# A chunked recurrence and its two-layer network: fewer transfers for N's blocks and y's last rows, one transfer queue, and another order of all steps

## The chip, the cores and the metric

The kernel runs on one core of one Trainium2 chip. The metric is the device time of one execution in microseconds (us). The engines' names in the profile are PE (TensorE, matrix products; PEld is its loading of weights), DVE (VectorE), ACT (ScalarE), POOL (GpSimd) and SP (SyncE, which here only issues transfers). SPq and ACTq are transfers as SyncE and ScalarE issue them.

## The reference

A recurrence over 768 time steps runs for 4 batches of 8 heads, each with a state of 40x40. Its outputs are laid side by side, 320 for each of the 3072 tokens, and go through two weight matrices with an exact GELU between them. The weights w_in and w_out arrive as 64-bit floats.

```python
for t in range(S):
    kt, vt, rt = (k[:, :, t], v[:, :, t], r[:, :, t])
    wt, at, bt = (w[:, :, t], a[:, :, t], b[:, :, t])
    y[:, :, t] = np.einsum('bhd,bhde->bhe', rt, state)
    Sa = np.einsum('bhde,bhe->bhd', state, at)
    state = state * wt[:, :, None, :] - np.einsum('bhd,bhe->bhde', Sa, bt) + np.einsum('bhd,bhe->bhde', vt, kt)
x = y.transpose(0, 2, 1, 3).reshape(B * S, H * D)          # 3072 x 320
h = x @ w_in                                               # 320 x 2048
out = (0.5 * h * (1.0 + erf(h / sqrt(2)))) @ w_out         # 2048 x 320
```

## The kernel before

**Chunks.** The 768 time steps are cut into 12 chunks of C = 64. Within a chunk the recurrence becomes matrix products and the inverse of a triangular 64x64 matrix for each head and batch; between chunks only the state is carried (`st`).

**Steps.** Each piece of a chunk's work is a generator, named by a few letters and the chunk. `w`, `a`, `b`, `k`, `v`, `r`, `vp`, `wq`, `bp` and `kp` load inputs (the last four, and `a` and `r` of the later chunks, by `fetch_pairs`); `logs`, `sums`, `wt` and `sc` make the decays; `ta`, `tb`, `tk`, `tv`, `tr` and `tn` turn operands; `N`, `RV`, `A` and `av` are products and masks; `QY` and `qk` add up the rows of y and the next state; `y`, `state`, `X`, `M`, `sa`, `saT` follow from them. `ph` (L1119) is x@w_in with Gelu and `po` (L1141, L1157) the product with w_out; they make up most of TensorE's time. `wi`, `wl` and `wo` load the weights, `ci` and `co` convert them to 32 bits on VectorE (L457 to L473) and ScalarE. `warm` and `begin` are filler products.

**The inverse.** For chunks 1 to 11 it goes this way. `N` takes the product, masks it (L676) and writes it to a DRAM tile (L715). `nb` (L777 to L785) loads its diagonal blocks of 32x32 into `Nb`, twice, for the two halves of the partitions. `inv` substitutes row by row on GpSimd (L799 and the line behind it) and stores the blocks' inverses in DRAM; `ft` (L822, L826) loads them into `Tt`; `corner` turns them on VectorE (L908) and multiplies; `joined` completes the 64x64 inverse. In chunk 0 the same is done by squaring on TensorE, VectorE and ScalarE: `sq` (L865 turns, L868 adds, L871 copies), `cornerd` (L876), `placed` and `joinedd`. `nb` has four transfers: both halves of the partitions for the first sixteen rows of every block, and then, after the next `yield`, both for the last sixteen.

**y.** `y(c)` multiplies the rows by the decays into `xt` (L1045), one head's 40 columns to 64 partitions. `ph` needs x in five pieces of 64 rows: four of them filled with 24 rows from the other half's heads (L1071, three transfers), and a fifth from the 16 rows of each head that are left over (L1076, eight transfers, each of 16 partitions with a stride of 4). For chunk 0 TensorE moves them. For chunk 11, by `MOVED_BY_ACT`, the transfers of one half (x = 1) are issued by ScalarE; all others of the kernel go through SyncE's queue, but for GpSimd's stores of the inverses from chunk 3 on.

**Order.** `ORDER` is a long list of tokens, written out. A token's name says which generator is to take its next step, the figures behind the colons in which pieces of PSUM. The loop at the end takes the tokens one by one:

```python
for token in ORDER.split():
    name, *at = token.split(":")
    places[:] = [int(x) for x in at]
    ...
    next(going[name], None)
```

Each engine, SyncE's queue among them, executes its instructions in the order in which the tokens produce them, and waits where an operand is not there. So the list decides what stands behind what on each engine.

Of the kernel before, what the change touches and what calls it, by code (L numbers as in the profile page):

```python
# [10 lines left out]
FP32 = mybir.dt.float32  # L11
# [8 lines left out]
WORDS_BY_ACT = False  # L20
COPIED_BY_ACT = (1, 2)
MOVED_BY_ACT = (11,)
# [8 lines left out]
w0 begin6 pads1 consts0 w1 tails1 b1 inv1 zeros1 begin6:0 logs0 zeros2 wi0 gaps0 b0 consts0 logs1 tails0 pads0 a0  # L31
consts0 sums0:1 gaps1 sums0:2 zeros0 v0 sums0 zeros4 warm6:3 pads3 pads2 sums1:0 zeros3 shifts0 sums0 sc0 a1 sums1:3
sums1 tb0:2 sums1 sc1 wi0 ta0:1 r0 tb0 ta0 tb1:3 N0:0 N0 tb1 wi0 ta1:2 k0 ta1 N0 tv0:1 sq1 v1 tv0 sq0 N1:3 sq0 sq0:0
sq1 sq0 sq1:2 k1 sq0 sq1 warm1:1 N1 sq1 sk0 ci0:0 wi0 sq1:0 N1 ci0 sq1 tr0:1 sq1 ci0 tk0:2 wi0 tk0 sk1 wi0 sq0:3 sq1
sq0 tr0 A0:2 ci1:1 sq1:0 sq0 ci1 sq1 sq0 nb1 sq1 A0 sq1 wi0 sq0:1 wi0 sq0 RV0:3 sq0 RV0 sq0 wl1 sq1:0 wl1 sq1 inv1 r2
sq0:2 sq1 sq1 sq0 tk1:1 sq0 sq0 sq1:3 tk1 w2 sq1 sq0:0 sq0 cornerd0 placed2 av0:2 ci2:2 placed3 cornerd0:3 ci1 ci2
inv1 nb1 placed1 warm0:1 cornerd0 wl0 ci3:0 wl0 av0 av0:0 r1 ci2 joinedd0:1 av0 joinedd0 tr2:3 placed0 joinedd0 tr2
warm2:2 wi1 a2 ci3 sa0:0 sa0 sa0:1 inv1 sa0 b2 warm5:2 ci4:1 ci9:2 ci4 QY0:3:0 logs2 ci4 k2 qk0 warm7:2 ci9 y0 warm3:1
wi1 state0 wi1 A1:2 wi1 A1 wi1 sums2:1 wi1 inv1 ci9 wo2 sums2:0 sums2 ci3 tv1:3 tv1 tr1:2 sc2 sums2 tn1:0 ci5:1 tn1
ta2:3 ta2 ci5 av1:1 tr1 ci5 sk2 inv1 y0:0 tb2:3 wi1 inv2 ci7:2 tb2 wo6 zeros6 y0:2 ci7 zeros7 y0 y0 tk2:3 av1 ci6:0  # L40
N2:2 ci6 N2 ft1 tk2 co3:1 ph0:0 ft1 ci6 wi1 ph0 corner1:0 N2 ci7 X1:1 corner1:2 corner1 ft1 ph0 X1 ph0:3 wo0 ci8:0
co2:2 ci8 RV1:2 RV1 nb2 warm4:1 ci8 joined1:0 wo9 joined1 wq3 ph0 co0:0 joined1 co0 inv2 ph0 co0 v2 ph0:1 co2 co3
co1:0 sa1:2 co1 sa1 w3 co1 saT1:0 saT1 co3 ph0 co2 wo4 ph0 inv2 ph0:3 co6:0 wt3:1 co6 co7:2 ph0 vp3 co7 ph0 co7
yy1:2:0 logs3 M1:1 M1 tv2:3 wt3 co6 wo8 sums3:1 nb2 sums3 wt3 QY1 zeros5 a3 inv3 tv2 qk1 co4:2 y1 wo15 po0:1 inv2
co5:0 y1 state1 co5 co4 po0 co5 RV2:3 wo10 A2:0 co4 y1 tn2:2 A2 tn2 co9:0 po0 ta3 co9 wt3 inv2 co15:2 bp3 po0 co9 co15
av2:0 co11:1 kp3 co8:0 co11 av2 co11 ph1:2 co8 co8 wo14 inv2 ph1 co10:1 tb3 co10 ph1 wo13 ph1:0 co10 a4 ph1 RV2 ph1
inv4 ft2 co14:0 ph1:2 ta3 co14 wo12 ft2 co14 ft2 N3:3 co15 X2:0 k4 X2 ph1 corner2:1 co13:0 corner2:0 N3 corner2 co13
co12:2 N3 po0 co13 co12 joined2:0 tables0 joined2 k3 joined2 po0 ta4 ph1 co12 sa2:3 nb3 tables0 saT2:0 tk3:1 b3 sa2
sk3 saT2 po0 r3 inv3 yy2:2:3 po0 po0 M2:0 po0 nb3 M2 po0 tv3 ph1:1 inv3 po0 tr3 wq4 ph1 sc3 QY2 w4 qk2 y2 po1:0 state2
bp4 inv3 po1 logs4 b4 A3:2 y2 A3 X3:3 wt4:0 po1 wt4 v3 ph1 wt4 po1 y2 inv3 wt4 po1 po1 ta4 kp4 po1 inv3 vp4 av3:2 tb4  # L50
av3 sums4:1 po1 X3 po1 RV3:2 v4 ws0 sums4 N4:3 N4 inv5 sk4 RV3 ph2:1 N4 sc4 tk4:2 ph2 ft3 ph2 ft3 ph2:3 ws3 nb4 ws1
nb4 ph2 corner3:1 ph2 ft3 ph2:2 inv4 a5 corner3:1 corner3 w5 ph2 ph2 joined3:3 joined3 r4 tn3:1 joined3 tn3 inv4
saT3:3 saT3 sa3:2 sa3 logs5 po1 ph2:1 ta5 bp5 yy3:3:2 M3:0 M3 inv4 tv4 ph2 ph2 tr4 wq5 QY3 qk3 po2:0 po1 sums5:0 sums5
y3 po1 po2:1 state3 y3 po2 inv4 wt5:2 RV4:0 po2:1 po2 wt5 k5 A4:2 po2 A4 tn4:3 y3 tn4 wt5 po2:1 tables1 wt5 po2 po2
inv4 kp5 av4:2 tb5 av4 X4:3 po2 ph3:2 sk5 X4 a6 po2 ta5 ph3 v5 RV4 N5:3 N5 ws2 po2:1 N5 po2 ft4 po2 ph3 ft4 ph3:0 ft4
corner4:0 nb5 tk5:2 ph3 vp5 ph3 corner4:3 ta6 corner4 inv5 nb5 po2 po2:1 po2 joined4:2 joined4 joined4 ph3:0 b5 saT4:3
saT4 sa4:1 r5 inv5 sa4 ph3 ph3 sc5 ph3:2 w6 yy4:3:1 M4:0 M4 tv5 ph3 inv5 ph3 tr5 wq6 QY4 logs6 po3:1 qk4 bp6 state4
po3:0 kp6 y4 po3 po3:2 wt6:0 A5:2 po2 sums6:1 A5 wt6 inv6 k6 inv5 sums6 wt6 y4 po3 wt6 po3 po3:3 po3 po3 tn5:2 y4 tn5
av5:1 tb6 RV5:0 po3 av5 po3 po3:2 ta6 b6 po3 inv5 po3 a7 N6:1 X5:3 N6 X5 N6 sk6 ph4:2 RV5 tk6:1 ph4 ph4 ft5 ta7 ph4:1
ft5 sc6 ft5 A6:3 corner5:0 nb6 r6 inv6 po3 po3:0 po3 corner5:2 A6 corner5 ph4 joined5:0 joined5 ph4 joined5 ph4:2 vp6  # L60
sa5:3 sa5 saT5:0 saT5 inv6 ph4 nb6 ph4 yy5:1:3 w7 M5:0 tr6 tv6 ph4:2 M5 wq7 ph4 inv6 ph4 QY5 v6 logs7 po4:2 qk5 po3 y5
bp7 po4:0 wt7:1 state5 wt7 po4 kp7 po4:0 av6:2 inv7 av6 y5 inv6 wt7 po4 po4 po4:1 wt7 po4 po4 v7 sums7:3 X6:2 y5 po4
ta7 sums7 tb7 po4 po4:0 po4 a8 X6 N7:3 inv6 N7 RV6:1 tk7:2 N7 ph5:2 po4 k7 ph5 ph5 ph5:3 ft6 nb7 ph5 ft6 ph5 nb7
corner6:0 ph5:0 RV6 ft6 inv7 corner6:2 po4 corner6 tn6:3 r7 tn6 po4:1 po4 joined6:2 ta8 joined6 joined6 ph5 inv7 vp7
ph5 sa6:3 sa6 saT6:1 saT6 ph5:2 po4 yy6:0:3 bp8 M6:1 M6 inv7 tr7 ph5 ph5 tv7 QY6 po5:1 wq8 qk6 y6 po5:1 state6 y6 po5
po5:2 inv7 po5 wt8:0 A7:2 y6 RV7:0 A7 wt8 tn7:3 RV7 tn7 wt8 vp8 inv7 po5 po5:1 po5 wt8 po5 X7:2 av7:0 inv8 av7 tb8 sk7
# [12 lines left out]
inv10 po8 wt11 po8:0 av10:2 bp11 po8 wt11 tr10 ph9:1 kp11 ph9 ta11 inv10 ph9 po8 tb11 ph9:0 b10 av10 ph9 X10 sk10 ph9
N11:1 N11 RV10:2 tk11:1 N11 ph9:3 ft10 RV10 ph9 ft10 ph9 nb11 ph9:0 corner10:0 ft10 sc10 w11 ph9 inv11 ph9 corner10:1  # L80
corner10 po9:2 vp11 po9:2 joined10:3 joined10 joined10 po9 nb11 sa10:0 inv11 sa10 r11 saT10:1 po9:1 saT10 tn10:3 tn10
po9 po9 po9:0 yy10:1:3 v11 M10:2 M10 tv11 po9 inv11 po9 po9 logs11 QY10 qk10 y10 po9 po9:2 y10 state10 po9 po9 X11:0
y10 sums11:1 sums11 A11:3 A11 inv11 po9 po9:2 po9 tn11:1 tr11 tn11 av11:3 po9 av11 RV11:2 X11 b11 inv11 RV11 ph10:1
k11 ph10 ph10 sc11 ph10:3 sk11 ft11 ph10 ft11 ph10 ft11 ph10:0 corner11:0 ph10 ph10 corner11:2 corner11 ph10:1
joined11:3 joined11 joined11 ph10 ph10 saT11:0 saT11 po10:2 po10:2 yy11:3:1 M11:0 M11 po10 po10:1 po10 QY11 po10 qk11
y11 po10:0 y11 po10 po10 y11 po10 y11 po10 po10:2 y11 y11 y11 po10 y11 po10 po10 po10:1 po10 po10 ph11:3 ph11 ph11
ph11:0 ph11 ph11 ph11:2 ph11 ph11 ph11:1 ph11 ph11 po11:0 po11:3 po11 po11:2 po11 po11 po11:0 po11 po11 po11 po11
po11:2 po11 po11 po11 po11:1 po11 po11
"""


@with_exitstack
def kernel(
    ctx: ExitStack,
    tc: tile.TileContext,
    r: bass.AP,
# [100 lines left out]

    raws = {}  # L200

    def rows(t):
        return t[:, :G * DM].rearrange("p (g h d) -> p g h d", g=G, h=H)
# [1064 lines left out]
```

## Time and profile before

| | |
|---|---|
| runs of the kernel (us) | 663.88, 664.77, 668.19; median 664.77 |
| span of the profiled execution (us) | 661.8 |
| own time of the profiled execution | not given apart from the span |
| TensorE busy (us) | 646.7 (98%), 13768 instructions |
| TensorE loading weights | 567.3 (86%) |
| VectorE, ScalarE, GpSimd busy | 416.0 (63%), 239.3 (36%), 367.7 (56%) |
| DMA | 300708 packets, 79.41 MB, mean 120 GB/s; SyncE's queue 58.3% of 16 engines' span |
| ScalarE's queue of transfers (y(11), x = 1) | 200 packets, 0.16 MB |

Rows of the timeline have start, duration, engine, line, operation, destination and sources, shapes and count, and in brackets the idle time before them and what ended it. Rows of the waits have the waiting engine and line, what it waited for, and then the total in us, how many times, and the longest. "issue" stands for idle time of an engine that waited for nothing that the profile shows. A row of the stretches has the length of the stretch, each engine's busy time with its number of instructions, the clock that TensorE was granted, the mean busy share of the 16 DMA engines and their GB/s.

### The profile page before, as it was taken

The numbers are of one execution on the slowest core, as the hardware profiler recorded it, in microseconds if no ns is written. First come the engines' busy times: TensorE is split into PE (matmuls) and PEld (weight loads), VectorE is DVE, ScalarE is ACT, GpSimd is POOL, SyncE is SP. The second block draws the span as 40 slices with busy tenths as digits, with TensorE's granted clock in tenths as the row PEclk, the third lists the DMA queues.
The fourth block names the chain that finished last, engine by engine and source line by source line (L and its number), as shares of the span: only waits on it lengthen the run. The fifth ranks groups of instructions, "written<-read, shape, count | busy, mean of one in ns | idle before, by whom it ended". The sixth has DMA issues, their size and how long they took to land.

```text
span 661.8 us, 30753 instructions
## 1 busy us (share of the span) xinstructions
PE 646.7 (98%) x13768; PEld 567.3 (86%) x13768; DVE 416.0 (63%) x536; ACT 239.3 (36%) x305; POOL 367.7 (56%) x799
## 2 busy tenths in 40 slices
PE   8889999999999999999999999999999999999997
PEld 4777788777778988998998998998988999998987
DVE  1778989976483874983863963863765674632313
ACT  4355646432424622522522422515253242232020
POOL 6158536706857837846838836847823874840000
PEclk9999999999999999999999999999999999999999
DMA  9989675696676476764775485675685465450100
GB/s 136 164 192 176 158 167 132 153 159 146 116 132 134 105 137 134 140 116 112 145 141 107 94 153 124 119 147 110 115 146 111 103 121 102 86 101 3 42 1 21
DMA packets 300708, 79.41 MB, mean 120 GB/s; under 512 B 288584, under 2 KB 293328, under 8 KB 300576
## 3 DMA queue, kind: packets, MB, share of 16 engines
q1 hardware_dynamic: 299512, 74.92, 58.3%
q0 software_dynamic: 864, 2.36, 1.8%
q8 instruction: 108, 1.77, 1.1%
q14 instruction: 24, 0.20, 0.1%
q10 hardware_dynamic: 200, 0.16, 0.1%
HBM read 64.09 MB, written 9.70 MB: 112 GB/s over the span
## 4 chain that ended last, share of the span: by engine, by line
PE 82%; DVE 8%; SPq 5%; issue 2%; DMA 1%; ACT 0%; DVEq 0%; ACTq 0%
PE duo L1119 29%; PE duo L149 25%; PE duo L1157 22%; PE duo L1141 4%; PE duo L557 2%; SPq L213 2%; SPq L227 1%; DVE conv L466 1%; SPq L1076 1%; DVE conv L472 1%; DMA spare<-in_a_dram 1%; DVE conv L458 1%; DVE conv L457 1%; DVE aT L588 1%; DMA rows<-in_b_dram 0%
## 5 line engine op out<-in xcount | busy, mean ns | idle before, releaser
L1119 PE MATMUL duo<-xt,w_in_sb 64*128 64x256 f32 x1920 | 218.8, 381 | 1.4 <-issue 1.4
L1119 PEld LDWEIGHTS duo<-xt,w_in_sb 64*128 64x128 f32 x1920 | 182.5, 187 | 23.9 <-issue 2.3
L799 POOL TENSOR_TENSOR tmp<-W,Nb 128x56 f32<-128x56 f32 (+22 forms) x155 | 71.8, 464 | 79.9 <-DMA Nb<-N 51.4
L1122 ACT ACTIVATE gt<-duo 128x1024 f32<-128x1024 f32 x48 | 49.2, 1025 | 143.0 <-PE duo L1119 132.1
L799 POOL TENSOR_TENSOR tmp<-rT,Nb 128x56 f32<-128x56 f32 (+22 forms) x155 | 70.2, 453 | 52.8 <-DMA Nb<-N 41.0
L1157 PE MATMUL duo<-w_out_sb,gt 128*128 128x160 f32 x640 | 93.3, 303 | 0.0
L1157 PEld LDWEIGHTS duo<-w_out_sb,gt 128*128 128x128 f32 x640 | 87.6, 190 | 2.4 <-issue 0.8
L801 POOL TENSOR_TENSOR W<-W,tmp 128x56 f32<-128x56 f32 (+22 forms) x155 | 71.8, 463 | 12.1
L801 POOL TENSOR_TENSOR rT<-rT,tmp 128x56 f32<-128x56 f32 (+22 forms) x155 | 68.4, 441 | 12.1
L1157 PE MATMUL duo<-extra,conv 128*128 128x160 f32 x320 | 46.0, 301 | 0.0
L1157 PEld LDWEIGHTS duo<-extra,conv 128*128 128x128 f32 x320 | 43.8, 190 | 1.4 <-issue 0.5
L1141 PE MATMUL duo<-w_out_sb,gt 128*128 128x320 f32 x128 | 36.9, 440 | 0.1
L1161 DVE TENSOR_TENSOR os<-os,duo 128x160 f32<-128x160 f32 x40 | 12.7, 318 | 31.9 <-PE duo L1157 28.0
L1141 PEld LDWEIGHTS duo<-w_out_sb,gt 128*128 128x128 f32 x128 | 23.6, 190 | 10.1 <-issue 0.5
L1164 DVE TENSOR_TENSOR conv<-gt 128x1024 f32<-128x1024 f32 x10 | 12.7, 1266 | 27.5 <-ACT gt L1122 27.5
L605 POOL TENSOR_TENSOR rows<-rows,w_tile 128x640 f32<-128x640 f32 x9 | 15.8, 1761 | 25.0 <-DMA Nb<-N 16.0
L676 DVE TENSOR_TENSOR SM<-duo,left_upper 128x1024 f32<-128x1024 f32 x11 | 13.4, 1221 | 24.4 <-PE duo L149 24.4
L931 DVE COPY Tt<-duo 32x512 f32<-32x512 f32 x11 | 7.6, 689 | 30.4 <-ACT Tt L931 30.3
L149 PE MATMUL duo<-rT,late 40*64 40x64 f32 x1472 | 26.1, 219 | 0.0
L149 PEld LDWEIGHTS duo<-rT,late 40*64 40x64 f32 x1472 | 23.7, 135 | 2.1 <-issue 2.1
L1122 ACT ACT_TABLE_LOAD x14 | 18.0, 1283 | 19.1 <-DVE os L1161 14.7
L1157 PE MATMUL duo<-extra,gt 128*128 128x160 f32 x160 | 23.9, 302 | 0.0
(222 smaller groups left out, 1092.0 us busy)
## 6 DMA issues: line engine op xcount, KB each, us to landing
Nb<-N SPq DMA_DIRECT2D x40, 128.0 KB
VR<-in_v_dram SPq DMA_DIRECT2D x24, 160.0 KB
out_dram<-os SPq DMA_DIRECT2D x48, 80.0 KB
rows<-in_b_dram SPq DMA_DIRECT2D x22, 160.0 KB
rows<-in_k_dram SPq DMA_DIRECT2D x22, 160.0 KB
w_out_sb<-in_moe_w_out_dram SPq DMA_DIRECT2D x5, 640.0 KB
w_tile<-in_w_dram SPq DMA_DIRECT2D x36, 80.0 KB
Tt<-inv SPq DMA_DIRECT2D x44, 64.0 KB
```

Of the source, the lines that this page charges most:

```text
L149: nc.tensor.matmul(o, lhsT, rhs, start=first, stop=True, skip_group_check=True)
L213: nc.sync.dma_start(out=t[half(e)].rearrange("p g h d -> p (g h) d")[:, :, :D], in_=rows_of(src, c, e))
L557: nc.tensor.transpose(pt[:, g, n], src(g, n), ident)
L605: (nc.gpsimd if c in SCALED_BY_POOL or c >= NB else nc.vector).tensor_tensor(to, raws.pop((c, "k")), t["rw"], ALU.mult)
L676: nc.vector.tensor_tensor(to, pt, upper.unsqueeze(1).to_broadcast([P, NBL, C]), ALU.mult)
L799: eng.tensor_tensor(t, W[:, :nr, j:j + 1].to_broadcast([P, nr, rest]), Nb[:, j:j + 1, j + 1:].to_broadcast([P, nr, rest]), ALU.mult)
L801: eng.tensor_tensor(W[:, :nr, j + 1:], W[:, :nr, j + 1:], t, ALU.add)
L1119: nc.tensor.matmul(pt[:, x, s], w_in_sb[half(x), kt, p * P:(p + 1) * P], xt[half(x), kt], start=kt == 0, stop=kt == NK - 1)
L1122: nc.scalar.activation(gt[:, 4 * q:4 * q + 4].rearrange("p (x s) t -> p x s t", x=2), pt, ACT.Gelu)
L1141: nc.tensor.matmul(pt[:, g], gt[:, f, g * P:(g + 1) * P], w_out_sb[:, f], start=f == 0, stop=f == NF - 1)
L1157: nc.tensor.matmul(pt[:, n, :DM // 2], l_[:, f], r_[:, f], start=f == 0, stop=f == NF // 2 - 1)
L1161: nc.vector.tensor_tensor(to, one_, other, ALU.add)
```

## The change

- `nb`, from chunk 3 on: two transfers instead of four, each with all rows of the blocks for one half of the partitions (4 KB a partition instead of 2).
- `y(c)` for chunks 1 to 10: the fifth piece goes by two transfers into a DRAM tile `last` (16 partitions of 4 KB each) and two back (64 partitions of 1 KB each) instead of eight within the on-chip memory. `y(11)` keeps its eight.
- `WORDS_BY_ACT` and `MOVED_BY_ACT` are gone. Loads and y's transfers go through `load`, whose queue is SyncE's unless a token begins with a star, and none does; so ScalarE's six transfers are SyncE's.
- `fetch_pairs`, `w`, `r`, `N` and `y` yield more often, between single transfers or pairs of them, so that the list can place these apart.
- `ORDER` is another list: 1467 tokens instead of 1334. The computing steps in it are the same, in other places. TensorE has 6976 products before and after; the transfers that SyncE and ScalarE issue go from 780 to 722.

```diff
-WORDS_BY_ACT = False
-MOVED_BY_ACT = (11,)
...
+    raws, queue = {}, [nc.sync]
...
+    def load(out, in_):
+        queue[0].dma_start(out=out, in_=in_)
...
     def nb(c):
...
         for z in range(2):
-            for par in range(2):
-                nc.sync.dma_start(out=Nb[par * n:(par + 1) * n, rows_of_blocks[z]], in_=blk[:, rows_of_blocks[z]])
+            for par in (range(2) if c < NT else (z,)):
+                rows_ = rows_of_blocks[z] if c < NT else slice(0, BL)
+                load(Nb[par * n:(par + 1) * n, rows_], blk[:, rows_])
             yield
...
     def y(c):
...
         for x in range(2):
             own, other = x * HP, (1 - x) * HP
-            eng = nc.scalar if x and c in MOVED_BY_ACT else nc.sync
             for to, n in ((0, NP - 1), (NP - 1, 1)) if x else ((0, NP),):
                 at = (to + x) % NP
-                eng.dma_start(out=xt[own + D:own + HP, to:to + n], in_=xt[other:other + REST, at:at + n])
-                if eng is nc.scalar:
-                    yield
+                load(xt[own + D:own + HP, to:to + n], xt[other:other + REST, at:at + n])
+            yield
+        if c == NCH - 1:
             for i in range(NP):
-                n = D - REST
-                eng.dma_start(out=xt[own + i:own + HP:NP, NP], in_=xt[other + REST:other + D, i])
-                if eng is nc.scalar and i < NP - 1:
-                    yield
-            yield
+                for x in range(2):
+                    own, other = x * HP, (1 - x) * HP
+                    load(xt[own + i:own + HP:NP, NP], xt[other + REST:other + D, i])
+                yield
+            return
+        last = dram.tile([2, D - REST, NP, TB], FP32, tag="last", name="last")
+        for x in range(2):
+            load(last[x], xt[x * HP + REST:x * HP + D, :NP])
+        yield
+        for x in range(2):
+            load(xt[half(x), NP], last[1 - x].rearrange("p i t -> (p i) t"))
+        yield
...
-        name, *at = token.split(":")
+        queue[0] = nc.scalar if token[0] == "*" else nc.sync
+        name, *at = token.strip("*").split(":")
```

The places in the list that the prediction speaks of: `b0` and `a0` stand ahead of `b1`, and `ta0` ahead of `tb0`; `ci0`'s third and `ci1`'s first piece stand behind the squaring (`sq0`, `sq1`) and the last of `ci9` ahead of it; the filler `warm3` stands in chunk 6 and `warm2` behind the last product of `po11` instead of in chunk 0; the mask of `N3` stands ahead of `corner2`; and between `qk1` and `ph1` TensorE has

```
qk1 y1 tk2 vp3 wt3 co9:1 A2:0 co9 inv3 y1 y1 po0 state1 tv2:1 tn2:2 A2 wt3 tv2 y1 tn2 ... po0 RV2:2 av2:1 wo8 k4 RV2 y1 X2:0 ph1:2
```

More of the change, by code (lines that the diff above doesn't have):

```diff
@@ L423, in wi @@
                     if m:
-                        (nc.scalar if x and WORDS_BY_ACT else nc.sync).dma_start(out=words[to:to + m, i], in_=words_from(first, [(4 * wd, m)], x, c))
+                        load(words[to:to + m, i], words_from(first, [(4 * wd, m)], x, c))
                 yield
@@ L431, in wl @@
         for x in range(2):
-            (nc.scalar if x and WORDS_BY_ACT else nc.sync).dma_start(out=words[half(x)], in_=words_from((1 - x) * D + REST, [(4 * wd, D - REST), (2 * D * 4 * wd, NP)], x, c))
+            load(words[half(x)], words_from((1 - x) * D + REST, [(4 * wd, D - REST), (2 * D * 4 * wd, NP)], x, c))
             yield
@@ L1130, in store @@
             row = (G * e + g) * S + c * C
-            nc.sync.dma_start(out=out[row:row + C], in_=oss[g][half(e)].rearrange("p z d -> p (z d)"))
+            load(out[row:row + C], oss[g][half(e)].rearrange("p z d -> p (z d)"))
     @step
```

187 lines of the change are left out of this document (92 added, 95 removed).

## Prediction

> **What bounds the kernel now.** I read the busy time of each engine first, cut into stretches where TensorE's waits change their kind, and then TensorE's waits. The last row is the sum over the span.
>
> ```profile
> core 0: us, PE busy (x) PEld busy (x) DVE busy (x) ACT busy (x) POOL busy (x), PEclk, DMA share, GB/s
> 0.00:1.54 1.54, 0.00 (x0) 0.00 (x0) 0.48 (x1) 0.00 (x0) 0.86 (x7) 1.00 0.00 0
> 1.54:47.30 45.76, 41.07 (x848) 32.23 (x848) 24.82 (x39) 20.26 (x27) 20.75 (x69) 1.00 1.01 166
> 47.30:142.20 94.90, 92.27 (x2053) 74.61 (x2049) 88.28 (x150) 50.13 (x66) 55.34 (x119) 1.00 0.78 165
> 142.20:613.50 471.30, 469.24 (x10521) 418.93 (x10521) 290.07 (x328) 163.75 (x205) 290.76 (x606) 1.00 0.60 117
> 613.50:657.40 43.90, 43.90 (x364) 41.56 (x356) 11.98 (x20) 5.17 (x8) 0.00 (x0) 1.00 0.06 16
> 657.40:661.80 4.40, 0.21 (x2) 0.00 (x0) 0.32 (x1) 0.00 (x0) 0.00 (x0) 0.89 0.30 75
> sum 661.80, PE 646.68 PEld 567.33 DVE 415.96 ACT 239.31 POOL 367.70; mean PE 107.78 PEld 94.55 DVE 69.33 ACT 39.88 POOL 61.28
> ```
>
> TensorE is busy for 646.68 of 661.80 us, at a granted clock of 1.00 in every stretch but the last. Its products are the same 6,976 before and after, so an order can win only two things: idle time of TensorE, and the cost of switching from one kind of product to another. Of the 15.1 us idle, 1.54 lie before the first instruction and 4.19 behind 657.40, in the last outputs' way out. Between them are 4.69 up to 47.30, 2.63 up to 142.20, 2.06 up to 613.50 and nothing in the last 43.90: **9.4 us that an order could remove**, 7.3 of them before 142.20. The four largest groups of waits say what ended most of them:
>
> ```profile
> PE duo L149 <- issue: 2.7, 4, 1.1
> PE duo L149 <- DVE w_in_sb L1220: 1.5, 1, 1.5
> PE duo L1119 <- issue: 1.4, 1, 1.4
> PE duo L149 <- ACT w_in_sb L871: 1.4, 2, 1.0
> ```
>
> Columns: total, times, longest. None of them is a transfer. What bounds the first 142 us beside TensorE is VectorE: 88.28 busy of 94.90 between 47.30 and 142.20.
>
> **The first 142 us in the new order.** Two VectorE instructions mark the stretch, the turn that ends chunk 0's squaring (L876) and the turn before chunk 2's corner (L908). The fence behind has TensorE's side: two filler steps, and the corner's product.
>
> ```profile
> 32.24 1.93 DVE L473 SCALAR_TENSOR_TENSOR w_in_sb<-conv 128x512 f32<-128x512 f32 x1
> 34.09 0.70 DVE L865 STREAM_TRANSPOSE Nb<-duo 128x512 f32<-128x512 f32 x1
> ...
> 46.62 0.71 DVE L876 STREAM_TRANSPOSE W<-w_in_sb 128x512 f32<-128x512 f32 x1
> ...
> 141.49 0.70 DVE L908 STREAM_TRANSPOSE conv<-Tt 128x512 f32<-128x512 f32 x1
> ```
>
> ```profile
> 61.98 1.98 PE L149 MATMUL duo<-cum_m,ident 128*128 128x512 f32 x4
> ...
> 144.48 0.75 PE L149 MATMUL duo<-conv,N 32*32 32x32 f32 x64
> ```
>
> Before, a squaring's turn stood behind a weight conversion of 1.93 (32.24), and with it the 1.0 us wait for L871. The new order moves two pieces of such conversions, 4.1 us in all, behind the squaring and one of 1.2 ahead of it, so I put the end of L876 at 44.0 instead of 47.3. Then VectorE has its 88.3 us, 2.8 of conversions (4.1 - 1.2), and N(3)'s mask, now ahead of L908, 1.2 for a pass over 1024 elements: 92.3. Without any idle time L908 ends at 136.3; with the 6.6 idle of before (94.90 - 88.28) at 142.9. I take 140.8, nearer to the later end, since a stretch in which VectorE also waits for transfers and for TensorE does not lose all of its idle time to another order. TensorE has two filler steps less ahead of the corner (1.98 for both): it comes there at 144.48 - 2.0 = 142.5 less whatever idle it avoids, and no earlier than L908. **The gain is 142.5 - 140.8 = 1.7 us; its bounds are -0.4 and +6.2.** One of the fillers put off returns in chunk 6. The other, `warm2`, now stands behind the last product of po(11), where TensorE has nothing to do for 4.19 us: **1.0 us gained**, bounds 0 and 1.0. Of the 2.06 us idle between 142.20 and 613.50 I let the new order keep all; bounds 0 and +2.1.
>
> **Fewer switches.** A run of products of x@w_in that is cut in two pays for it:
>
> ```profile
> 307.40 2.43 PE L1119 MATMUL duo<-xt,w_in_sb 64*128 64x256 f32 x20
> ...
> 311.79 4.59 PE L1119 MATMUL duo<-xt,w_in_sb 64*128 64x256 f32 x40
> ```
>
> Twenty more products cost 4.59 - 2.43 = 2.16, so a run costs 0.27 on top; entering it costs up to 0.2 more by the overlap of neighbours. The new order leaves and enters ph and po about 4 times less often (84 to 81, 85 to 81): 4 x 0.25 = **1.0 us gained**, bounds 0 and 1.8.
>
> **N's blocks.** For chunks 3 and up two transfers of 4 KB rows replace four of 2 KB:
>
> ```profile
> 246.50 1.73 SPq L784 DMA_DIRECT2D Nb<-N  x2
> 248.28 4.03 SPq L224 DMA_DIRECT2D v_pairs<-in_v_dram  x8
> 252.41 2.12 SPq L784 DMA_DIRECT2D Nb<-N  x2
> ```
>
> ```profile
> POOL tmp L799 <- DMA Nb<-N: 92.4, 9, 18.2
> ```
>
> The bytes are the same and two issues (1.73 to 2.12) go. But the inverse on GpSimd, which could begin with the first sixteen rows, now needs both transfers: up to 2.1 us later for the second issue. GpSimd already idles 92.4 us in these waits, and the new order, its steps summed at their durations in this trace, leaves 61 to 66 us of TensorE work between N and the corner where it left 54 to 63 (chunk 8 alone loses 1.1). VectorE, which waits for the inverse next, has slack in those chunks (290.07 busy of 471.30). I take **0**; bounds -0.5 and 0. If that cover went, the corner, and joined, X and the state behind it, would come late by what is missing.
>
> **y's last rows.** For y(1) to y(10) the eight transfers of 16 KB become two writes into DRAM and two reads back. That adds a wait on the path, the reads behind the writes.
>
> The first fence has the small transfers, the next two TensorE's pieces that cover them in the new order, the last three the pieces of the chain.
>
> ```profile
> 122.20 2.44 SPq L1076 DMA_DIRECT2D xt<-xt  x4
> ```
>
> ```profile
> 119.11 1.11 PE L149 MATMUL duo<-aT,kT 40*64 40x64 f32 x64
> 120.15 1.09 PE L557 MATMUL duo<-ident,st 128*128 128x128 f32 x8
> 121.36 4.57 PE L1141 MATMUL duo<-w_out_sb,gt 128*128 128x320 f32 x16
> ```
>
> ```profile
> 108.17 1.97 PE L149 MATMUL duo<-ident,VR 128*64 128x128 f32 x32
> ```
>
> ```profile
> 613.62 1.29 DVE L1045 TENSOR_TENSOR xt<-duo,wpT 128x512 f32<-128x512 f32 x2 [1.09 <-PE duo L149]
> ```
>
> ```profile
> 614.93 0.82 SPq L1071 DMA_DIRECT2D xt<-xt  x1
> ```
>
> ```profile
> 29.25 2.16 SPq L715 DMA_DIRECT2D N<-spare  x4
> ...
> 35.04 1.09 SPq L784 DMA_DIRECT2D rows<-N  x2
> ```
>
> A small issue takes 2.44 / 4 = 0.61, so the 58 issues that the whole change saves are 35 us of SyncE's queue. The new way lasts 1.3 (L1045) + three shifts at 0.82 + two writes at 0.61 + a landing L + two reads at 0.61 + L = 6.2 + 2L. TensorE's work between qk(c) and ph(c) covers it, and 0.86 more, since ph begins with eight products (at 2.16 / 20 = 0.108) on rows that are there. That cover is least at c=1: 4.57 (two parts of po) + 1.97 (tv) + 1.09 (tn) + four products at 1.1 (A, RV, av, X), which with the neighbours' overlap is 11.7; then, by the same sum over the new order's steps, 12.8 at c=10, 14.2 at c=8 and 17.4 or more at the rest. The first stall comes at L = (12.5 - 6.2) / 2 = 3.2. No row shows this round trip; the nearest bound L from above. N's four writes into DRAM were all issued at 31.41 and read from 35.04 on (3.6, other work included), and y(11)'s last small transfer, below, left its queue at 622.23 for products that began at 624.66 without a wait (2.4, or 3.3 with the 0.86). From below it is 0. I take L between 2 and 3, so **no stall**, and a loss of 0; the bounds are 0 and, at L = 6, 13.2 us. The reads wait in SyncE's queue; behind them stand loads for later chunks, ten times at most 3 us, less than the 35 saved.
>
> The Trainium skill ("DMA: Bandwidth & Descriptors", Anatomy of one DMA) puts a fixed 2.0 us on a transfer, most of it the write's receipt, heaviest towards HBM, and its section Latency and other measured facts adds that an HBM access rises from 0.2 to 2 us at high load. By that L would be 2 to about 4: nothing at 2, and at 4 some 1.7 us at c=1 and 0.5 at c=10.
>
> **y(11) by SyncE alone.** ScalarE's six issues, the last four of them here, join SyncE's:
>
> ```profile
> 619.03 3.20 ACTq L1076 DMA_DIRECT2D xt<-xt  x4
> 624.66 2.65 PE L1119 MATMUL duo<-xt,w_in_sb 64*128 64x256 f32 x22
> ```
>
> ScalarE's last ended at 622.23 (619.03 + 3.20). SyncE alone needs three shifts at 0.82 and eight at 0.61 from 614.93 on: 622.3, ahead of ph(11) at 624.66. **0**, bounds -1.5 and +0.5.
>
> **Sum.** 1.7 + 1.0 (the filler) + 1.0 (the switches) + 0 + 0 + 0 = 3.7 us: a span of 658.1. The page gives no time of its own for the profiled execution; the runs' median, 664.77, stands 2.97 over the span. So the forecast is **661.1 us**.
>
> **Rivals.**
> *Slower: the round trip through DRAM is late.* At L = 5 the way lasts 16.2: ph(1) stalls 3.6, ph(10) 2.5, ph(8) 1.1. At L = 6 it is 18.2: 5.6 + 4.5 + 3.1 = 13.2, and the time 661.1 + 13.2 = 674.3. It costs something from L = 3.2 and decides (over 1% slower) from L = 5.5. For it: two transfers in series where there was one, at a DMA share of 0.78 around c=1. Against it: the 3.6 above, measured at a share of 1.01.
> *Faster: VectorE never idles up to L908.* Then 6.2 there, 1.0 from the filler and 1.8 from the switches: a span of 652.8, a time of 655.8. For it: 7.3 us of idle lie in that stretch and the waits for L1220 and L871 end on what surrounds the squaring. Against it: VectorE also waits for loads, which the DMA share of 1.01 does not let come earlier.
> *The order gives nothing.* L908 ends at 142.9 with the idle time of before (-0.4), the filler gives 1.0 and the switches 0 to 1.0: 663.2 to 664.2. For it: the same transfers feed the same first chunks. Against it: the 1.0 us wait behind a conversion is gone in any case.
>
> **How the numbers follow.** The forecast's case has a chance of 0.48, an order that gives nothing 0.18, the late round trip 0.20, and the busy VectorE 0.14. The forecast's own range is 657 to 665 by the bounds of its small terms; for 8 in 10 I reach towards both rivals, 655 to 672. About 1% (6.6 us) is what a measurement of this kernel can tell from no change: below 658.1 is faster, above 671.4 slower. The busy VectorE counts as faster, with some of the forecast's low end (0.05): 0.19. The late round trip counts as slower only past L = 5.5: 0.15. The rest, 0.66, is the same.
>
> **What would show it.** Right: the end of L908 for chunk 2 near 141, TensorE's idle time between its first instruction and there about 5 to 6 instead of 7.3, no wait of L1119 for a transfer into xt, the reads of `last` issued 2 to 3 us behind the writes, ph(11) starting without a wait, GpSimd's wait for Nb grown by no more than 20 us. Wrong: waits of L1119 on xt at c=1, 8 or 10 (the slower rival), a corner (L149 with conv) that waits for VectorE's L908 past chunk 3, an L908 at 137 (the faster), or a sum of TensorE's busy time that moves by more than 2 us although the products are the same.

## The result and the profile after

The changed kernel took 668.83 us (median of 20 executions, 664.84 to 673.52); the kernel before, run beside it, 665.89 (20 executions, 661.85 to 669.27). The ratio is **1.0045, 95% interval 1.0025 to 1.0065**: slower by 3 us, within the 1%, where 3.7 us less was forecast. The interval leaves out both no change and a gain. Repeated on another chip the ratio was 1.0029 (1.0002 to 1.0055).

The profiled execution of the changed kernel took 671.06 us with a span of 669.4, so 1.7 lie outside the span. It was one of its slower executions, and the profiled one of before, with a span of 661.8, one of its quicker ones: the two profiles lie 7.6 us apart, the medians 2.9. So the stretches show where time goes, but more of it than a usual execution loses.

The stretches of the changed kernel, with the columns as before (the first stretches cut at 94.00 as well):

```profile
1.54:47.30 45.76, 45.17 (x968) 34.92 (x970) 24.79 (x42) 22.30 (x31) 16.95 (x56) 1.00 1.00 162
47.30:94.00 46.70, 41.10 (x818) 33.45 (x814) 43.87 (x68) 22.93 (x29) 36.16 (x75) 0.89 0.98 171
94.00:142.20 48.20, 47.95 (x1102) 39.57 (x1100) 42.67 (x77) 26.84 (x34) 23.87 (x58) 1.00 0.75 160
142.20:613.50 471.30, 466.20 (x10326) 416.55 (x10324) 283.73 (x326) 161.43 (x202) 292.56 (x605) 1.00 0.64 120
613.50:665.10 51.60, 51.11 (x573) 48.33 (x572) 16.75 (x24) 7.81 (x13) 2.19 (x1) 1.00 0.06 14
665.10:669.40 4.30, 0.85 (x2) 0.02 (x1) 0.32 (x1) 0.00 (x0) 0.00 (x0) 0.91 0.31 76
```

The same cut of the kernel before:

```profile
47.30:94.00 46.70, 44.82 (x1068) 34.88 (x1066) 41.49 (x65) 25.35 (x33) 26.39 (x51) 1.00 0.82 175
94.00:142.20 48.20, 47.44 (x987) 39.73 (x985) 46.79 (x86) 24.78 (x33) 28.95 (x69) 1.00 0.73 156
```

Up to 47.30 TensorE's idle time falls from 4.69 to 0.59: a gain of 4.1 us, more than was hoped for. It is lost at once: from 47.30 to 94.00 the idle time is 5.60 instead of 1.88, and the granted clock is 0.89 instead of 1.00. From 142.20 on another 5.10 us stand idle where 2.06 did, and 0.49 behind 613.50 where there was nothing. A second trace of the changed kernel (`changed_again`, span 668.7) has the same shape in other sizes: idle for 0.54 us up to 47.30, for 4.42 up to 94.00 at a clock of 0.93, and for 8.41 between 142.20 and 613.50. TensorE's waits in the changed kernel:

```profile
PE duo L151 <- issue: 4.8, 2, 3.1
PE duo L151 <- DVE aT L590: 2.5, 3, 1.6
PE duo L151 <- DVE w_in_sb L1226: 1.5, 1, 1.5
PE duo L151 <- ACT turned L997: 1.3, 1, 1.3
PE duo L1125 <- issue: 1.0, 2, 0.5
PE duo L1163 <- ACT avs L761: 1.0, 1, 1.0
PE duo L151 <- DVE SM L678: 0.5, 1, 0.5
```

No transfer into xt is among them: y's round trip is covered. The two long ones by "issue" stand in the middle of a run of small products, and the clock halves behind them:

```profile
49.72 1.70 PE L151 MATMUL duo<-VR,nT 64*64 64x104 f32 x28 [1.69 <-issue]
...
80.43 0.34 PE L151 MATMUL duo<-rT,late 40*64 40x64 f32 x7 [3.11 <-issue]
```

```profile
50.00:54.00 4.00, 4.00 (x53) 2.25 (x53) 3.93 (x6) 3.45 (x5) 3.53 (x7) 0.60 0.99 134
...
80.00:84.00 4.00, 3.57 (x81) 3.13 (x83) 3.96 (x5) 1.74 (x2) 3.38 (x6) 0.69 0.83 127
84.00:88.00 4.00, 4.00 (x20) 3.22 (x22) 3.93 (x9) 1.84 (x2) 1.12 (x4) 0.50 1.05 254
```

What ended these stalls is in the trace's DMA records. TensorE's program arrives in packets of 16 KB (queue q8, 108 packets for its 27,536 instructions, as many as no other engine has, some 6 us apart). One landed at 48.40 and one at 78.97; TensorE went on 1.32 and 1.46 us later. All 20 traces together have 67 such stalls of 0.5 us or more, and each ended 1.2 to 2.0 us after a packet had landed, with a median of 1.48. **So TensorE stood for its own program.** Why the packet was late is not shown; in the four stalls above 3 us it started only when TensorE had stopped already.

Three times in this execution (at 50.8, 81.5 and 330.7 us; for 3.4, 6.8 and 3.4 us) the clock is at half; in the second trace it is once, for 6.8 us behind a stall of 2.10. TensorE's busy time of 652.4 instead of 646.7 goes with that: with the new list at a full clock (`repaired`, below) it is 646.5. The Trainium skill ("TensorE: Matmul & The Clock Gate", Part 1: The HAM clock gate) has the gate judge windows of about 3.4 us, and the lengths here agree with it. Over its 20 executions the changed kernel's clock averaged 0.996, and the kernel before had 0.998 (23 executions beside `changed_again`). The four executions of the changed kernel at 1.0 took 667.1 us on average, all 20 took 668.9; by that some 1.7 of its 3 us go with the clock, as an estimate.

### The profile page after: what moved, and what is told of

Same layout as the page of the kernel before. It is cut to its first block, busy times and chain, and to the rows that moved or that the text cites. A ratio compares the mean times of both kernels' runs of the same rounds, so it can differ in the third digit from the quotient of the medians.

```text
span 669.4 us, 30662 instructions
## 1 busy us (share of the span) xinstructions
PE 652.4 (97%) x13768; PEld 572.8 (86%) x13768; DVE 412.6 (62%) x536; ACT 241.3 (36%) x306; POOL 372.7 (56%) x799
## 3 DMA queue, kind: packets, MB, share of 16 engines
q0 software_dynamic: 864, 2.36, 2.1%
## 4 chain that ended last, share of the span: by engine, by line
PE 88%; DVE 4%; SPq 3%; issue 2%; ACT 1%; DMA 1%; DVEq 0%; ACTq 0%
PE duo L1125 32%; PE duo L151 27%; PE duo L1163 22%; PE duo L1147 5%; SPq L214 3%; PE duo L559 2%; DMA gt<-in_moe_w_in_dram 1%; DVE aT L590 1%; DVE SM L678 0%; DMA v_pairs<-in_v_dram 0%; DVE conv L474 0%; DVE w_out_sb L475 0%; DVE conv L468 0%; ACT avs L761 0%; DVE Nb L845 0%
## 5 line engine op out<-in xcount | busy, mean ns | idle before, releaser
L1125 PE MATMUL duo<-xt,w_in_sb 64*128 64x256 f32 x1920 | 222.1, 383 | 1.0 <-issue 1.0
L1125 PEld LDWEIGHTS duo<-xt,w_in_sb 64*128 64x128 f32 x1920 | 184.8, 188 | 25.5 <-issue 2.3
L801 POOL TENSOR_TENSOR tmp<-W,Nb 128x56 f32<-128x56 f32 (+22 forms) x155 | 68.7, 443 | 50.3 <-DMA Nb<-N 38.5
L1163 PEld LDWEIGHTS duo<-w_out_sb,gt 128*128 128x128 f32 x640 | 89.3, 193 | 3.4 <-ACT avs L761 1.6
L803 POOL TENSOR_TENSOR rT<-rT,tmp 128x56 f32<-128x56 f32 (+22 forms) x155 | 74.1, 478 | 12.1
L607 POOL TENSOR_TENSOR rows<-rows,w_tile 128x640 f32<-128x640 f32 x9 | 15.7, 1748 | 57.7 <-ACT w_tile L524 33.9
L1147 PEld LDWEIGHTS duo<-w_out_sb,gt 128*128 128x128 f32 x128 | 23.6, 190 | 9.7 <-issue 0.5
L678 DVE TENSOR_TENSOR nT<-duo,left_upper 128x1024 f32<-128x1024 f32 x12 | 14.6, 1219 | 20.1 <-PE duo L151 20.0
```

The lines of the kernel that those rows point to most:

```text
L607: (nc.gpsimd if c in SCALED_BY_POOL or c >= NB else nc.vector).tensor_tensor(to, raws.pop((c, "k")), t["rw"], ALU.mult)
L678: nc.vector.tensor_tensor(to, pt, upper.unsqueeze(1).to_broadcast([P, NBL, C]), ALU.mult)
L801: eng.tensor_tensor(t, W[:, :nr, j:j + 1].to_broadcast([P, nr, rest]), Nb[:, j:j + 1, j + 1:].to_broadcast([P, nr, rest]), ALU.mult)
L803: eng.tensor_tensor(W[:, :nr, j + 1:], W[:, :nr, j + 1:], t, ALU.add)
L1125: nc.tensor.matmul(pt[:, x, s], w_in_sb[half(x), kt, p * P:(p + 1) * P], xt[half(x), kt], start=kt == 0, stop=kt == NK - 1)
L1147: nc.tensor.matmul(pt[:, g], gt[:, f, g * P:(g + 1) * P], w_out_sb[:, f], start=f == 0, stop=f == NF - 1)
```

## The experiments

Ratios are to the kernel before, run beside each on the same chip, with 95% intervals. Names like av(6) are steps and chunks.

**Order alone, transfers alone.** `order_alone` is the new list with the transfers of before (in short: the remarks are not in the code, and y(11)'s split between the two queues is not shown):

```diff
-                load(Nb[par * n:(par + 1) * n, rows_], blk[:, rows_])      # nb: two, whole rows
+                load(Nb[par * n:(par + 1) * n, rows_of_blocks[z]], blk[:, rows_of_blocks[z]])   # four
-            load(last[x], xt[x * HP + REST:x * HP + D, :NP])               # y: through DRAM
+                load(xt[own + i:own + HP:NP, NP], xt[other + REST:other + D, i])                # eight direct
```

> The changed kernel's order with the transfers of before: nb's four transfers, y's eight direct ones for all chunks, half of y(11)'s by ScalarE. If the order is what costs (my theory: TensorE's program fetched late between 47 and 94 us, its clock halved behind these waits, and some waits on ScalarE and VectorE in later chunks), the time stays near the changed kernel's: 667 to 670. If the transfers cost (the round trip through DRAM, or N's blocks as a whole), it falls to 663 or below, since the first 47 us had gained 4.5.

`transfers_alone` is the reverse: the list of before with the new transfers.

> The order of before with the new transfers: nb's two, y's last rows through DRAM (both writes behind all three shifts at the place of the first token, both reads at the second), y(11) by SyncE alone. If the order is what costs, the time is that of before within 2 us: 664 to 668. If the round trip costs, there are waits of the products of x@w_in for a transfer into xt, and the time is 670 or more.

They took 676.02 (1.0136, 1.0098 to 1.0175) and 676.75 (1.0157, 1.0118 to 1.0196). Each half alone is three times as bad as both together. The new order is slow with the transfers of before, so "the order costs" and "the transfers cost" are both too simple, and each part was tried by itself. The time of `transfers_alone` is no price of the transfers, as the next kernel shows.

**nb in the old order.** `nb_alone` has nb's two transfers in the kernel before and nothing else.

> The kernel before with nb's two transfers alone. With all new transfers in the old order, SyncE stood 13.3 + 13.1 us at nb until GpSimd was done with the inverse before it, which no row of before shows; behind nb stand the loads of later chunks. If that wait is what makes the new transfers slow in the old order, this kernel shows most of it: 5 to 9 us slower than before, with SyncE's waits at nb for GpSimd back. If the round trip costs, it is within 2 us of before.

681.68 (1.0219, 1.0169 to 1.0269): the largest single loss, and more than expected. SyncE's queue in it, and GpSimd's and VectorE's instructions, around chunk 10:

```profile
526.72 2.27 SPq L213 DMA_DIRECT2D rows<-in_k_dram  x2
536.95 0.47 SPq L785 DMA_DIRECT2D Nb<-N  x1
537.52 2.12 SPq L227 DMA_DIRECT2D v_pairs<-in_w_dram  x4
```

```profile
535.65 1.27 POOL L800 TENSOR_TENSOR tmp<-W,Nb 128x128 f32<-128x128 f32 x1
...
540.51 0.42 POOL L800 TENSOR_TENSOR tmp<-W,Nb 128x135 f32<-128x135 f32 x1 [3.05 <-DMA Nb<-N]
```

```profile
543.01 1.25 DVE L561 STREAM_TRANSPOSE conv<-v_pairs 128x1024 f32<-128x1024 f32 x1 [6.35 <-DMA v_pairs<-in_w_dram]
```

```profile
SPq L785 <- POOL rT L802: 14.0, 4, 5.2
SPq L785 <- POOL tmp L800: 13.0, 2, 7.9
```

```profile
PE duo L1158 <- DVE nT L676: 4.5, 1, 4.5
...
PE duo L149 <- DMA VR<-in_v_dram: 3.0, 3, 2.1
```

SyncE stands from 528.99 to 536.95, and it does not stand for the inverse before, as the expectation had it, but for the first sixteen steps of the same one: the step with 128x128 elements is the sixteenth, that with 128x135 the seventeenth, and it waits 3.05 us for the transfer. The list of before has such steps between its two tokens of nb, 8 of them in chunks 3, 5, 9 and 11 and 16 in chunks 6 and 10; these are the four and the two waits of L785. In the kernel before that is sound, since the first token brings the first sixteen rows for both halves of the partitions. In `nb_alone` it brings all rows for the lower half only. So `nb_alone`, and `transfers_alone` as well, leave out the upper half's new rows in these steps: they work on the rows of the chunk before. **The 15 us are the price of a list that does not fit this nb, not of larger transfers.**

Behind nb in the queue stand loads, among them `v_pairs`, which the kernel before issued at 517.75. VectorE turns them late (6.35 us of idle time), and TensorE waits 4.5 us for VectorE. In this trace TensorE is idle for 25.6 us, 10.5 more than before, and busy for 654.2, 7.5 more, at a mean clock of 0.990.

The new list has both tokens of nb side by side and ahead of the first step from chunk 3 on. In the changed kernel's trace no group of SyncE's waits for GpSimd at L214, the line of all its loads, is longer than this:

```profile
SPq L214 <- POOL tmp L801: 2.3, 6, 0.5
```

**y in the old order.** `y_alone` has the round trip through DRAM alone.

> The kernel before with y's last rows through DRAM alone (chunks 1 to 10; nb and y(11) as before). If nb is what costs in the old order, within 2 us of before, and no wait of x@w_in's products for a transfer into xt. If the reads' wait for the writes' landing (11.1 us of SyncE's time with all new transfers) holds up the loads behind it, 3 us or more slower.

663.38 (0.9961, 0.9928 to 0.9995): a small gain, not a cost. Where it comes from is not shown. SyncE's wait for the landing, over nine reads:

```profile
SPq L1077 <- DMA last<-xt: 14.5, 9, 2.9
```

**y and nb in the new order.**

> The changed kernel with y's eight direct transfers for chunks 1 to 10, nb and y(11) as in the change. With all transfers of before the new order took 676, and TensorE waited 2.4 us for transfers into xt. If y's way is what the new order is laid for, this is slower than the changed kernel by 4 to 7 us and waits for xt appear; if nb is, within 1.5 us of it.

> The changed kernel with nb's four transfers of before. The new list puts both tokens of nb next to each other, late, where the inverse before is done with its tile. If the two transfers only fit that list, the time stays within 1.5 us of the changed kernel's; if the two transfers gain by themselves there, it is 3 us or more slower.

With the eight direct transfers (`new_order_old_y`) 673.74 (1.0127, 1.0096 to 1.0159), and TensorE waits 1.6 us for xt: in the new order y's new way is worth about 0.8%, and 1.4% with nb's four transfers (1.0136 for `order_alone`, which has y(11) split as before too, against the next ratio). With nb's four transfers (`new_order_old_nb`) 665.71 (0.9999, 0.9976 to 1.0022), which was not expected: nb's two transfers cost the new order. With y's old way that cost is not seen: 1.0127 with two stands beside 1.0136 with four, from 6 executions each. The two kernels with y's new way were then set side by side on one chip.

> The changed kernel itself, on one chip with the next one. It stood at 1.0045 of the kernel before (1.0025 to 1.0065) and the same with nb's four transfers, on another chip, at 0.9999 (0.9976 to 1.0022). If nb's two transfers cost in the new order, this stands again 0.3 to 0.6% above the next kernel; if the difference was the chip's, within 0.2%.

> The changed kernel with nb's four transfers of before, beside the changed kernel on one chip: near 1.000 of the kernel before if nb costs, within 0.2% of the changed kernel if it does not.

669.19 (1.0029) against 665.51 (0.9983); the means of their executions lie 3.4 us apart (95%: 2.0 to 4.8, from 12 each). **nb's two transfers cost the new order, with y's new way, 3.4 us.** The inverse does start later with them: in chunk 7, 4.5 and 4.8 us behind nb's first issue in the two traces of the changed kernel, and 3.4 in the two with four transfers. One place where that counts can be seen. The instruction of GpSimd behind chunk 7's inverse falls into a pass of VectorE:

```profile
384.11 3.50 DVE L616 SCALAR_TENSOR_TENSOR nT<-nT,kT 128x1024 f32<-128x1024 f32 x1
387.53 1.21 DVE L590 TENSOR_TENSOR aT<-aT,wpT 128x1024 f32<-128x1024 f32 x1
```

```profile
384.92 1.60 POOL L607 TENSOR_TENSOR rows<-rows,w_tile 128x640 f32<-128x640 f32 x1
```

```profile
388.89 1.16 PE L151 MATMUL duo<-aT,nT 40*64 40x64 f32 x64 [1.55 <-DVE aT L590]
```

With nb's four transfers (`old_nb_beside`) GpSimd is through before VectorE starts:

```profile
378.31 1.23 DVE L616 SCALAR_TENSOR_TENSOR nT<-nT,kT 128x1024 f32<-128x1024 f32 x1
```

```profile
376.46 1.75 POOL L607 TENSOR_TENSOR rows<-rows,w_tile 128x640 f32<-128x640 f32 x1
```

The pass takes 3.50 instead of 1.23 us, and TensorE waits 1.55 for what stands behind it. It is 3.2 to 3.5 in all four traces with two transfers and their list unmended there (waits 1.1 to 1.6), and 1.23 in both with four and the same list (no wait). The Trainium skill ("GPSIMD Engine Reference", 1. Specifications) says that GpSimd shares its way to the on-chip memory with VectorE and contends with instructions that have two inputs there; the pass has two, and the trace agrees. The other 2 us of the 3.4 are not located.

Two kernels ask what in nb it is. `nb_rows_swapped` takes the four transfers and issues the last sixteen rows first; `nb_four_wide` takes four with 4 KB rows for 32 partitions each.

> The changed kernel with nb's four transfers of before (665.7 with them), but the last sixteen rows issued first and the first sixteen, on which the inverse's start waits, last. The transfers are the same; only the inverse starts later, by one pair's issue (about 1.2 us). If the later start is what nb's two transfers cost in the new order, the time rises by 2 to 3 us to the changed kernel's; if the shape of the transfers is (4 KB rows), it stays at 665 to 666.

> The changed kernel with nb in four transfers as before in number, but with whole 4 KB rows for 32 partitions each, so that the inverse's start waits for all four. A later start alone changed nothing (ratio 0.9999 with the rows swapped, as with the transfers of before; 1.0045 for the changed kernel). If the 4 KB rows cost, it stays at 1.003 to 1.006; if the number of transfers does (two, less spread), it falls to 0.998 to 1.002.

668.98 (0.9999, 0.9967 to 1.0031) and 667.34 (1.0000, 0.9972 to 1.0029). Chunk 7's inverse starts late here too (4.8 and 4.1 us behind the first issue), and GpSimd and VectorE collide as well: with the rows swapped the pass takes 2.03 us, without a wait behind it, and the one of chunk 8 takes 3.03, with a wait of 0.94; with the wide rows the next pass (L590) takes 2.57, with a wait of 0.64. Neither a later start nor wide rows alone bring the loss back. That points to two transfers instead of four, but these intervals touch the changed kernel's, so it is not settled, and the collision at chunk 7 is not shown to be what the 3.4 us are made of.

**The waits of the later chunks.** `repair_only` moves three tokens of the changed list (pieces of three of its lines):

```diff
-po4:3 po4 po4 po4 inv6 tn6 av6:2
+po4:3 po4 tn6 po4 po4 inv6 av6:2
-N8:2 N8 kp8 inv7 vp8 N8 N8 RV7:3 X7:1
+RV7:3 N8:2 N8 kp8 inv7 vp8 N8 N8 X7:1
-av11:2 po9 po9 po9 av11
+av11:2 po9 av11 po9 po9
```

> The changed kernel with three tokens of the later chunks moved (the copies of tn(6) and av(11) ahead of a copy of po on ScalarE, N(8) behind RV(8)), the first 640 KB load left in its place. With both edits the time was 665.55, with the load alone 667.48. If the waits in the later chunks are the larger part of what the new order loses, this run stands 2 to 3 us below the changed kernel, near 666; if the stall at 77 us and the clock behind it are, it stands within 1 us of it.

665.50 (0.9988, 0.9964 to 1.0012), 0.57% below the changed kernel's ratio of 1.0045 and 0.41% below the repeated one of 1.0029. In the changed kernel ScalarE's copies of tn(6) and av(11) stand behind a copy of po that waits for TensorE:

```profile
327.52 0.29 ACT L1193 COPY os<-duo 128x160 f32<-128x160 f32 x1 [2.36 <-PE duo L1163]
327.71 1.02 ACT L997 COPY turned<-duo 128x1024 f32<-128x1024 f32 x1
```

```profile
328.79 1.14 PE L151 MATMUL duo<-VR,nT 64*64 64x40 f32 x64 [1.30 <-ACT turned L997]
```

TensorE has ended po's products at 327.49 and stands until the copy behind po's copy gives its piece of PSUM free. This wait, the one at av(11) and the 1.55 us above are gone from the trace of `repair_only`. So the new list adds waits in the later chunks that the list of before had not.

**The seam.** `halves_new_old` follows the new list (with a load moved, next paragraph) up to chunk 4 and then the list of before.

> The new order (with the 640 KB load moved) up to chunk 4's products, then all that is left in the order of before, with nb from chunk 7 and y from chunk 5 as before. If the new order gains in the first half and loses in the second (in the changed kernel, chunk 5 to 11 took about 8 us more than before, by TensorE's waits on ScalarE and VectorE), this is faster than before by 2 to 4 us and faster than the changed kernel by 5 or more. If the loss is spread evenly, or comes from a clock that falls at random, it is within 2 us of the changed kernel.

678.63 (1.0159): the expectation failed at the seam, where w(6) was loaded late:

```profile
299.71 1.34 PE L150 MATMUL duo<-w_tile,cum_m 64*64 64x320 f32 x8 [10.84 <-ACT w_tile L500]
303.30 2.08 PE L1141 MATMUL duo<-xt,w_in_sb 64*128 64x256 f32 x8 [2.24 <-ACT w_tile L523]
```

13.1 us of waits made by the cut, with 13.7 us of halved clock from 293 on. Behind it TensorE stood for 1.1 us in two waits to the end, which fits the finding on the later chunks but does not replace a clean run.

**Fillers and the load ahead of the stall.**

> The changed kernel with the two fillers back in the first chunks: one ahead of av(0)'s second half (where TensorE stood 1.7 us at 48), one ahead of RV(1) (where it stood 3.1 us at 77). If the fillers are what kept the clock up, no window of the clock is halved before 100 us and the time falls by 2 to 4 us. If TensorE's program was late because the DMA was full, the stalls stay or move by a fill's 1 us, and the time stays within 1.5 us of the changed kernel's.

> The changed kernel with one load moved: the first 640 KB of w_out's words, issued at 70.7 us ahead of N(2)'s store, now behind it. If bulk loads in front of TensorE's program make it late, the 3.1 us stall at 77 shrinks to below 1.5 us and the halved clock behind it goes in most executions: 2 to 3 us faster than the changed kernel. If the stall has another cause, it stays at about 3 us and the time moves by less than 1.

> The new order with four tokens moved: the 640 KB load; the copy of tn(6) on ScalarE ahead of po(4)'s copy, behind which av(6) waited 1.3 us at 327; N(8) behind RV(8), since it waited 1.55 us at 387; the copy of av(11) ahead of po(9)'s, behind which po(9) waited 1.0 us at 580. If these waits are what the second half loses, they are gone from TensorE's idle time and the time falls by 3 us against the run with the load alone moved (667.5 there). If other work takes their place, by less than 1.

With the fillers back: 670.66 (1.0053, 1.0024 to 1.0083), nothing gained, though no window of the clock was halved in its trace. With the load moved: 667.48 (1.0006, 0.9975 to 1.0037), with load and tokens moved (`repaired`) 665.55 (0.9991, 0.9962 to 1.0021), no better than the tokens alone. The stall at 77 us was 0.2 us, and none, in those two traces, and 1.3 to 3.4 in most with the load in its place; but it was 1.8 in the next kernel, load moved, and none in the one after, load in place. The load is not shown to be what makes TensorE's program late.

**The filler, and the best version.** `y_filler_last` is `y_alone` with warm(2) behind the last product; `best` is the new list with nb's four transfers, the three tokens and the load moved; `best_load_back` the same without the load.

> The kernel before with y's last rows through DRAM (663.4 alone) and one filler, warm(2), moved behind the last product. The prediction put 1.0 us on that filler. If it lies on the path, the time falls by 1 us against y's transfers alone; if the filler stood where TensorE would have waited anyway, or kept its clock, it stays or rises by up to 2.

> The new order with what the runs point to: y's last rows through DRAM, nb's four transfers of before, the three tokens of the later chunks moved, and the first 640 KB load behind N(2)'s store. If the gains add up (nb 0.45%, the tokens 0.55%, the load 0.1 to 0.4%), it stands at 0.992 of the time before, 660 to 661.5; if they overlap, at 663 to 665.

> The version that was fastest so far (0.9924: y through DRAM, nb's four transfers, three tokens of the later chunks moved) with the first 640 KB load back in its old place. In that version's trace TensorE still stood 1.8 us at 77.6, with the load moved. If the load in front is not what makes TensorE stand there, the ratio stays within 0.2% of 0.9924; if it is, it rises by 0.3% or more.

663.31 (0.9958, 0.9941 to 0.9976): the filler is worth nothing that can be told beside 0.9961. `best` 665.44 (0.9924, 0.9894 to 0.9955, from 7 executions; the two stood beside different runs of the kernel before, so their ratios compare and their times do not), `best_load_back` 663.78 (0.9941, 0.9916 to 0.9967). **Both beat the kernel before and the changed one**; new list, new y, old nb. But y's new way alone, in the list of before, stands at 0.9961 and 0.9958, and these intervals overlap with theirs: the runs do not show that the new list gains anything beyond it.

## Why the prediction was wrong

The sum went wrong in four terms, by the prediction's own steps, and one thing was no term at all.

- **N's blocks, taken as 0 with bounds -0.5 and 0: measured -3.4 us** (2.0 to 4.8) in the new order with y's new way. The later start came (1.1 to 1.4 us in chunk 7, "up to 2.1" by the prediction), and GpSimd's idle time was to cover it. The step that failed asks only who waits for the inverse. GpSimd has other work behind the inverse, that work came late too, and at chunk 7 it ran into a pass of VectorE for which TensorE then waited 1.1 to 1.6 us. What the rest of the 3.4 is stays open.
- **"Of the 2.06 us idle between 142.20 and 613.50 I let the new order keep all; bounds 0 and +2.1": it became 5.10** (8.41 in the second trace), and moving three tokens gave 0.41 to 0.57% back (2.7 to 3.8 us with what hung on them). A bound below zero was missing: a list that is wholly new can bring waits of its own, and the term was bounded as if it could only take them away.
- **The first 142 us, +1.7 with bounds -0.4 and +6.2.** L876 ended at 42.8 (44.0 forecast), and by 47.30 4.1 us were gained. But the corner's product began at 145.34 instead of 144.48, with L908 at 144.07:

```profile
42.09 0.70 DVE L876 STREAM_TRANSPOSE W<-w_in_sb 128x512 f32<-128x512 f32 x1
...
144.07 0.71 DVE L908 STREAM_TRANSPOSE conv<-Tt 128x512 f32<-128x512 f32 x1 [1.03 <-DMA Tt<-inv]
```

  L908, which the prediction set as the floor of the corner, did not set the time: the product began 0.56 us behind its end without a wait for it, as it had 2.29 behind it in the kernel before. VectorE itself waited for the inverse there. TensorE's own stalls (1.69 and 3.11, for its program) and the clock behind them ate the gain, and how much they eat changes from execution to execution. In five traces of the new list with y's new way whose clock stayed at 1.00 up to 94 us (`wo0_later`, `old_nb_beside`, `fillers_back`, `repaired`, `nb_rows_swapped`) the corner began at 140.6 to 142.6, near the 140.8 forecast; in five with 0.93 to 0.96 there at 139.8 to 145.1; in three with 0.89, the changed kernel's among them, at 145.3 to 147.7. Five traces with the list of before have it at 144.1 to 145.6. (The conversions that move, 4.1 - 1.2, are 2.9 and not 2.8; that is 0.1 us.)
- **The clock was no term.** The prediction read 1.00 in every stretch and kept it, and it held that an order can win or lose only idle time and switches. "A sum of TensorE's busy time that moves by more than 2 us" was named as a sign of error, and it came: +5.7, and +2.1 in the second trace.
- **y's last rows, taken as 0 with bounds 0 and -13.2: a gain**, 0.39% in the old order and about 0.8% in the new. The landing L was near the forecast: in `y_alone` the reads began 1.6 to 3.3 us behind the end of the writes' issue, and no product of the changed kernel waited for xt. The fixed 2.0 us that the prediction took from the Trainium skill ("DMA: Bandwidth & Descriptors", Anatomy of one DMA) is given there for transfers that GpSimd issues; these were SyncE's. Failed was the bound at 0 from above: the prediction counted 35 us of SyncE's issue time saved and gave it no worth. That the gain comes from there is likely, and not shown.

Right: y(11) by SyncE alone costs nothing (the last of its issues ended at 630.74, and ph(11) started without a wait at 632.14). GpSimd's waits for `Nb` did not grow; they fell to 79.1 us. The switches came out as good as nothing: at a full clock TensorE was busy for 646.5 us with the new list (`repaired`) and 646.7 before, so 1.0 us was too much. The filler behind the last product, another 1.0, gave no gain that was measured.

Of the rivals none was it. The late round trip fell. The busy VectorE fell. The likeliest case had the right class, within 1%, and the wrong sign. That 668.8 lies within 655 to 672 is luck: the forecast's own range ended at 665, and the upper part was added for a late round trip that did not come. It is luck as well that `best_load_back`, with 0.9941, ends near the 3.7 us that were forecast: 0.4% comes with y's new way alone, which was to bring nothing.

## What to carry to other kernels

A hand-written order is fitted to its transfers, so a transfer that looks cheaper in itself can cost where it stands. Take a change of both apart in both orders, but look first at which steps a list has between the parts of a transfer: if the parts are cut another way, those steps may read what has not come yet, and the run times another program. When something on an engine with slack starts later, ask what that engine does next, and beside whom. When a whole order is exchanged, the bound on each stretch has to reach below zero, since new waits come with new neighbours, and one profile of each kernel does not give the size of a 3 us difference.

## What the runs showed of the hardware

- TensorE can stand for its own program: 67 stalls of 0.5 to 3.35 us without a wait in 20 traces, each ended 1.2 to 2.0 us after a 16 KB packet of its program had landed.
- A halved clock can follow short idle times of TensorE, and does not always: 0.75 us (`wo0_later`, at 500), 0.89 (`new_order_old_nb`, at 49), 1.30 (changed kernel, at 327), 1.69 and 3.11 were each followed within 3 us by 3.4 or 6.8 us at half, while 1.30 at the same place in `changed_again`, 1.41 in the kernel before and 2.36 in `old_nb_beside` were not. The Trainium skill ("TensorE: Matmul & The Clock Gate", Why this matters for your kernels) warns of idle gaps above some 3 us; here a quarter of that was enough at times.
- A pass of VectorE with two inputs can stand for the whole of a GpSimd pass. In eight traces in which GpSimd's L607 and VectorE's L616 or L590 overlapped at chunk 7, VectorE's pass ended 1.08 to 1.10 us after GpSimd's; alone it takes 1.23 (L616) or 1.21 (L590). GpSimd's pass was no longer for it (1.60 to 1.81 us, and 1.75 without an overlap in `old_nb_beside`).
- Execution to execution the changed kernel varies by 8.7 us (664.84 to 673.52), and its granted clock from 0.989 to 1.0; one profile is one draw from that.
